# A drain written in another order, 54 transposes of the identity in it, and single PSUM banks behind it

## The chip, the cores and the metric

The kernel runs on one core of one Trainium2 chip. The metric is the device time of one execution in microseconds (us). Five engines work side by side, each through its own instructions in its own order: TensorE (PE, whose weight loads show as PEld), VectorE (DVE), ScalarE (ACT), GpSimd (POOL) and SyncE (SP), which here only issues DMAs. Matmul results lie in PSUM, 8 banks of 128 x 512 fp32; everything else lies in SBUF.

## The reference

Two attentions per head, then a mixture of experts with soft routing. N = 8 x 576 = 4608 rows of 512 come out of the attention, 32 slots go to 8 experts, 4 slots each.

```python
def sm_attn(qq, kk, vv):
    s = scale * np.matmul(qq, kk.transpose(0, 1, 3, 2))
    s = s - np.max(s, axis=-1, keepdims=True)
    a = np.exp(s)
    a = a / (np.sum(a, axis=-1, keepdims=True) + 1e-09)
    return np.matmul(a, vv)
p_packed = sm_attn(p, k, v)                # 8 batches, 8 heads, 32 x 64
x = sm_attn(q, p_packed, p_packed)         # 8, 8, 576 x 64 -> 4608 x 512
...
logits = x @ phi                           # 4608 x 32
d = np.exp(logits - logits.max(0, keepdims=True))
d /= d.sum(0, keepdims=True) + 1e-09       # softmax over the 4608 rows
slot_input = (d.T @ x).reshape(E, S_per_e, D)
for e in range(E):
    slot_out[e] = np.maximum(slot_input[e] @ w1[e], 0.0) @ w2[e]
c = np.exp(logits - logits.max(1, keepdims=True))
c /= c.sum(1, keepdims=True) + 1e-09       # softmax over the 32 slots
return (c @ slot_out.reshape(n_slots, D)).astype(np.float32)
```

## The kernel before

The attention runs in 8 steps i: double batch dd = i // 2 (two batches side by side on the 128 partitions) and head group g = i % 2. x is never formed: a step leaves the second attention's weights `a2`, and the logits come out of them and a small product of the packed values and phi. The names in the order, with the lines of the profile:

- `S2` and the scores s (L418, L430, a step's 72 matmuls); `MS`, `E2`, `Z`, `N2` the softmax: maximum (L457), difference (L458), exponent (L467), sum and reciprocal (L473 to L475), product (L480, on POOL or DVE); `MP` (L361) makes the small product with phi.
- `A2P` transposes `a2` on PE (L491) and `A2T` copies it (L502, L504); `LG` the logits lp (L518), `LT` keeps or adds them (L532, L535). The last step's softmax and transposes are cut in two (`E20`, `E21`, `A2P0`, `A2P1` and so on).
- Per double batch the softmax over rows runs on, with a running maximum and sum: `F1` maximum mt (L541), `F2` its transpose mx (L548), `F2d` new maximum m and difference dm (L555 to L568), `F3` two broadcasts my (L575, L583), `F3d` nmg (L588), `F3x` exponents dL and al (L594, L597), `F4d` two DVE transposes dz and rw (L604, L606), `F4` the sum mz (L611), `F5` the logits' transposed copy into `L_sb` (L614), `GZ` the running sum z_run and its rescaling of S_run (L624 to L636).
- `GR`: 36 matmuls gr of dz with `a2` (L654; a row of the order counts 18, the trace 36). `RTa` and `RTd` copy the result to rt on ACT and DVE (L667, L669), `GT` 16 more (L677), `GB` the product rb with the heads' mask (L688), `GS` (L710), `GSA` adds to S_run (L730). For the last double batch the sum goes to xz (L921), the experts' input.

`ORDER` (from L825) is a hand-written table of these names; inside `manual_schedule` each engine among PE, DVE, ACT and POOL keeps the order in which the table issues its work, and waits there in place. So an instruction that waits holds back all that follows it on its engine. SP is not in it: loads go out when their slot of the ring (14 slots of 1 MiB, and 7 extra ones) is free; weights are 32 pieces of 1 MiB. A step's `S2.7`, `F5.3` and `GR.3` also free the room for some of them, and the later ones wait for the experts to use up earlier ones.

Behind xz the experts run: `layer1a` (hp, L982, on 8 weight pieces for four experts), `hidden` (hs, L999, L1001), `layer1b` (ht, L1010), `layer2` (so, L1031); the last expert in halves (`last2`, sb, L1108), then sr (L1121, L1129) and sh (L1131, L1132). Beside them the combine weights are made from `L_sb`: maximum cm (L937), difference, exponent (L946), sum (L949), reciprocal, product (L952); nine groups `cp` of four transposes (L1062) bring them into the form cT. At the end 36 outputs: a matmul op (L1145, L1162), a copy to ob or ot by ACT (L87) or DVE (L90), and stores over SP (L1164, L1169, L1178). `evac` gives a copy to the engine with less on its account. PSUM is dealt out by pools: `pair` gives two banks under one name, `bank` one. In the attention `psm` holds one pair and `prs` three; behind it `psa` holds two pairs (hp, sb, sr, op), `pso` one bank (so), `pstr` three (ht, cp).

Behind the last step a drain is left: the logits of the last step, the softmax and gr of double batches 2 and 3.

Of the kernel before, what the change touches and what calls it, by code (L numbers as in the profile page):

```python
# [20 lines left out]
def pack_attention_soft_moe(  # L21
# [522 lines left out]
    def f2(dd):  # L544

        x = du[dd]
        bm = x["bm"] = pair(prs, f"mx_{dd}")[:, 0]
        nc.tensor.transpose(bm[0:1, 0:P], x["mt"], ident)  # L548
# [190 lines left out]
    def load_w(pool, lay, e, c):  # L739
# [92 lines left out]
        XQA.2 PREP.2 N2.1 MP.2 MXb.3 MM.2 S1a.3 EXb.3 MXa.3 QC.2 A2P.1 XQC.2 EXa.3 KT1.4 A2T.1
        S2.2 KT0.4 QE.3 AP.3 MT.2 MS.2 AT.3 A1T.3 LG.1 A1U.3 QC.3 PPM.3 XQC.3 E2.2 LT.1 F1.0
        F2.0 PPN.3 QA.3 F2d.0 QB.3 XQA.3 Z.2 F3.0 S1a.4 XQB.3 S1b.4 F3d.0 MXa.4 N2.2 F3x.0 F4d.0
        EXa.4 PT.3 MXb.4 PPT.3 F4.0 GR.0 QE.4 KT0.5 EXb.4 PRP.3 MP.3 RTa.0 AP.4 MM.3 PREP.3
        RTd.0 GZ.0 A1T.4 GT.0 KT1.5 S2.3 GB.0 GS.0 MT.3 AT.4 GSA.0 A2P.2 F5.0 A1U.4 MS.3 PPM.4
        A2T.2 QC.4 LG.2 E2.3 PPN.4 QB.4 LT.2 QE.5 Z.3 PT.4 XQC.4 XQB.4 QA.4 XQA.4 S1a.5 N2.3
# [373 lines left out]
```

## Time and profile before

| what | value |
|---|---|
| time, median of 3 runs | 240.16 us (239.95 to 242.99) |
| the profiled execution: time, span | 241.48 us, 239.7 us |
| PE busy | 192.1 us, 80% of the span |
| DVE, ACT, POOL busy | 137.5, 89.7, 31.2 us |
| DMA moved | 72.84 MB, mean 304 GB/s |
| HBM read, written | 62.98 MB, 9.44 MB |
| mean granted clock of PE | 0.876 |

The page gives busy times per engine and in 40 slices, the chain of work that ended last, and groups of instructions by line. A matmul's time is given up to its modelled end, so a PE that looks busy may be waiting inside its row of matmuls. [...]

### The profile page before, as it was taken

The page shows a single profiled execution, that of the slowest core. Times are in us where ns is not written, and L with a number is a line of the kernel's source. Part 1 is how long each engine was busy: PE and PEld are TensorE (multiplying, and loading weights), DVE is VectorE, ACT ScalarE, POOL GpSimd, SP SyncE. Part 2 cuts the span into 40 slices and gives each one's busy share as a digit, 9 for nine tenths or more (in the row PEclk, how much of TensorE's full clock was granted, in tenths as well). Part 3 has the DMA queues.
Part 4 walks back from the last instruction along what each step waited for, and adds up shares of the span by engine and source line. Part 5 has one row for each costly group of instructions (what it writes and reads, how often), then busy time and mean ns, then how long its engine had stood idle before and what let it go on. Part 6 is the DMA issues. An engine that isn't in the chain of part 4 may idle for free.

```text
span 239.7 us, 6484 instructions
## 1 busy us (share of the span) xinstructions
PE 192.1 (80%) x2795; PEld 128.6 (54%) x2795; DVE 137.5 (57%) x280; ACT 89.7 (37%) x174; POOL 31.2 (13%) x42
## 2 busy tenths in 40 slices
PE   0569977899879999979998627874999999688960
PEld 0247666777649777769786515772233344233320
DVE  2563786678596689767776486396312634433240
ACT  2041736374472473643667332102020010444520
POOL 6103000521060030020223010100030000000000
PEclk9999999999997999979999995757899999855555
DMA  5999999999999999995592990086499992278767
GB/s 155 385 338 349 390 391 270 390 389 326 345 389 391 391 406 407 407 374 187 198 355 72 424 383 5 0 299 228 130 421 428 418 415 118 72 282 347 298 278 304
DMA packets 27037, 72.84 MB, mean 304 GB/s; under 512 B 6400, under 2 KB 6656, under 8 KB 24192
## 3 DMA queue, kind: packets, MB, share of 16 engines
q1 hardware_dynamic: 27008, 72.42, 81.7%
q8 instruction: 22, 0.36, 0.6%
q14 instruction: 7, 0.06, 0.1%
HBM read 62.98 MB, written 9.44 MB: 302 GB/s over the span
## 4 chain that ended last, share of the span: by engine, by line
PE 52%; DMA 18%; DVE 14%; ACT 8%; issue 3%; SPq 1%; POOL 0%; DVEq 0%; ACTq 0%
DMA pn<-in_p_dram 8%; PE gr L654 7%; PE hp L982 7%; DMA k<-in_k_dram 6%; PE op L1145 6%; PE so L1031 5%; PE m L297 5%; PE s L430 4%; PE s L229 4%; DMA q<-in_q_dram 4%; PE a2p L491 3%; PE ap L263 2%; DVE ob L90 2%; ACT ob L87 2%; DVE kT L212 2%
## 5 line engine op out<-in xcount | busy, mean ns | idle before, releaser
L229 PE MATMUL s<-kT,pT 32*32 32x288 f32 x512 | 20.7, 458 | 9.2 <-DVE kT L212 8.7
L1145 PE MATMUL op<-sh,cT 128*128 128x512 f32 x35 | 23.1, 744 | 2.9 <-DVE ob L90 1.3
L480 POOL TENSOR_TENSOR a<-a,z 128x1152 f32<-128x1152 f32 (+1 forms) x8 | 15.9, 1992 | 61.7 <-DVE nmg L588 19.0
L212 DVE STREAM_TRANSPOSE kT<-k 128x1152 f32<-128x1152 f32 x16 | 21.4, 1358 | 0.2
L297 PE MATMUL m<-v,a1T 64*64 64x128 f32 x576 | 19.8, 291 | 0.7 <-ACT a1T L287 0.4
L250 ACT ACTIVATE a<-s,nm 128x576 f32<-128x576 f32 x16 | 11.9, 742 | 19.5 <-DVE nm L240 13.4
L297 PEld LDWEIGHTS m<-v,a1T 64*64 64x64 f32 x576 | 17.5, 144 | 3.1 <-issue 1.2
L240 DVE TENSOR_REDUCE nm<-s 128x1 f32<-128x576 f32 x16 | 12.0, 755 | 11.1 <-PE s L229 11.1
L1145 PEld LDWEIGHTS op<-sh,cT 128*128 128x128 f32 x35 | 9.8, 279 | 15.8 <-ACT ob L87 7.3
L386 PE MATMUL qp<-ident,q 128*128 128x128 f32 x128 | 16.7, 276 | 1.2 <-issue 1.2
L229 PEld LDWEIGHTS s<-kT,pT 32*32 32x32 f32 x512 | 9.0, 111 | 15.6 <-DVE kT L212 9.6
L90 DVE COPY ob<-op 128x512 f32<-128x512 f32 (+1 forms) x13 | 8.6, 670 | 14.0 <-PE op L1145 13.5
L87 ACT COPY ob<-op 128x512 f32<-128x512 f32 (+1 forms) x20 | 11.4, 575 | 13.5 <-PE op L1145 11.7
L654 PE MATMUL gr<-a,dz 128*64 128x128 f32 x144 | 16.4, 398 | 0.0
L982 PE MATMUL hp<-w,xz 128*32 128x512 f32 x128 | 16.0, 649 | 0.5 <-DVE xz L921 0.5
L430 PE MATMUL s<-ppT,qT 128*64 128x64 f32 x512 | 16.3, 222 | 0.1
L391 ACT COPY qT<-qp 128x1024 f32<-128x1024 f32 x16 | 15.9, 1021 | 0.7 <-PE qp L386 0.6
L386 PEld LDWEIGHTS qp<-ident,q 128*128 128x128 f32 x128 | 14.0, 141 | 3.3 <-issue 2.7
L654 PEld LDWEIGHTS gr<-a,dz 128*64 128x64 f32 x144 | 15.2, 206 | 1.1 <-issue 0.9
L430 PEld LDWEIGHTS s<-ppT,qT 128*64 128x64 f32 x512 | 15.6, 138 | 0.2 <-ACT a L250 0.2
L491 PE MATMUL a2p<-ident,a 128*128 128x128 f32 x64 | 9.7, 296 | 5.5 <-POOL a L480 4.5
L457 DVE TENSOR_REDUCE mx<-s 128x32 f32<-128x1024 f32 (+1 forms) x9 | 9.9, 1096 | 6.0 <-PE s L430 6.0
(144 smaller groups left out, 283.0 us busy)
## 6 DMA issues: line engine op xcount, KB each, us to landing
w<-in_moe_w_dram SPq DMA_DIRECT2D x31, 1024.0 KB, 10.7
k<-in_k_dram SPq DMA_DIRECT2D x16, 576.0 KB, 8.4
v<-in_v_dram SPq DMA_DIRECT2D x16, 576.0 KB, 10.3
q<-in_q_dram SPq DMA_DIRECT2D x16, 576.0 KB, 11.6
out_dram<-ob SPq DMA_DIRECT2D x7, 1024.0 KB, 3.9
pn<-in_p_dram SPq DMA_DIRECT2D x16, 64.0 KB, 8.0
w<-in_moe_w_dram SPq DMA_DIRECT2D x2, 512.0 KB, 16.9
out_dram<-ot SPq DMA_DIRECT2D x2, 512.0 KB, 5.3
```

The source lines that it names most:

```text
L87: nc.scalar.copy(dst, src)
L212: nc.vector.transpose(st[i]["kT"][:, b2].rearrange("p a t x r -> p (a t x r)"), kts[i][:, b2].rearrange("p a x -> p (a x)"),)
L229: nc.tensor.matmul(ps[32 * c : 32 * c + 32, u, 0:HALF], pTs[dd][rs, b2, g, a, x], kT[rs, b2, a, :, x, :], start=(x == 0), stop=(x == 1),)
L297: nc.tensor.matmul(s["m"][64 * b2 : 64 * b2 + 64, y, 0:P], s["a1T"][rs, t, 64 * b2 : 64 * b2 + 64], vt[rs, b2, :, t * D : (t + 1) * D], st ...
L386: nc.tensor.transpose(tp[:, o : o + P], qts[i][:, b2, a, j * P : (j + 1) * P], ident)
L391: nc.scalar.copy(flat(qT(i)[:, 8 * b2 : 8 * b2 + 8]), st[i][f"qp{b2}"])
L430: nc.tensor.matmul(pv[64 * b2 : 64 * b2 + 64, j, h], s["qT"][:, 8 * b2 + 4 * a + j, R * y : R * y + R], ppT[:, b2, h], start=True, stop=True,)
L480: eng.tensor_tensor(a2, a2, st[i][f"z{t0}"].unsqueeze(3).broadcast_to([P, n, 4, NS]), op=ALU.mult)
L491: nc.tensor.transpose(s["ap2"][:, t * P : (t + 1) * P] if t < 8 else s["lp"][:, 1, 0:P], s["a2"][:, t].rearrange("p h s -> p (h s)"), ident,)
L654: nc.tensor.matmul(x["gb"][64 * c : 64 * c + 64, g * P : (g + 1) * P], dz[:, t].rearrange("p b s -> p (b s)"), a2[:, t].rearrange("p h s - ...
L982: nc.tensor.matmul(hp[nh][32 * a : 32 * a + 32, :], xzf[:, (4 * e + a) * NSLOT : (4 * e + a + 1) * NSLOT], w1s[e, a // 2][:, a % 2, nh * 5 ...
L1145: nc.tensor.matmul(op, cT[:, o, :], sh, start=True, stop=True)
```

## The change

1. `ORDER`. For double batches 0 and 1, `F3` to `F4d` go ahead of `QB`, `Z` and the next `MX`, and `GR` ahead of `F4`. For double batch 2, `F2` to `F4d` go ahead of `MP.7` to `MT.7`, `GR.2` right behind `S2.7`, `GT.2` ahead of `A2P0.7`, `GS.2` ahead of `LG.7`, all of it ahead of `F1.3`; `mz` takes its bank from `psm`. For double batch 3, `GR.3` goes ahead of `F4.3` and `GZ.3`.
2. `fill(x, o)`: PE transposes of the identity into a part of a PSUM bank that nobody reads, at six places (`GT.2` 12, `F2.3` 11, `F3.3` 7, `GR.3` 12, `GT.3` 6, `GS.3` 6). Those at GR, GT and GS write the second bank of the pair whose first bank gr uses.
3. The maximum cm of the combine weights is tied behind xz.
4. hp, sb, sr and op take single banks out of `pstr`, which grows from 3 to 7; `psa` goes.

```diff
+    FILL = {("GT", 2): 12, ("F2", 3): 11, ("F3", 3): 7, ("GR", 3): 12, ("GT", 3): 6, ("GS", 3): 6}
+
+    def fill(x, o):
+        for _ in range(FILL.get(x, 0)):
+            nc.tensor.transpose(o, ident, ident)
...
         bm = x["bm"] = pair(prs, f"mx_{dd}")[:, 0]
+        fill(("F2", dd), bm[:, P : 2 * P])
...
         bm = x["bn"] = pair(prs, f"my_{dd}")[:, 0]
+        fill(("F3", dd), bm[:, 0:P])
...
-        x["zp"] = pair(prs, f"mz_{dd}")[:, 0, 0:NSLOT]
+        if dd == ND - 2:
+            mz = psm.tile([P, 2, 512], F32, tag="m", name=f"mz_{dd}")
+        else:
+            mz = pair(prs, f"mz_{dd}")
+        x["zp"] = mz[:, 0, 0:NSLOT]
...
-            x["gb"] = pair(prs, f"gr_{dd}")[:, 0]
+            gp = pair(prs, f"gr_{dd}")
+            x["gb"], x["gf"] = gp[:, 0], gp[:, 1, 0:P]
+            fill(("GR", dd), x["gf"])
...
     def gt(dd):
+        fill(("GT", dd), du[dd]["gf"])
...
         x["gs"] = x["gb"]
+        fill(("GS", dd), x["gf"])
...
-        GT.2 F2d.3 F3.3 GB.2 GS.2 F3d.3 F3x.3 GSA.2 F4d.3 F4.3 F5.3 GZ.3 GR.3 RTa.3 RTd.3 GT.3
+        F2.3 F2d.3 F3.3 F3d.3 F3x.3 F4d.3 F5.3 GR.3 F4.3 GZ.3 RTa.3 RTd.3 GT.3 GB.3 GS.3 GSA.3
...
-        psa = ctx.enter_context(tc.tile_pool(name="psa", bufs=2, space=psum))
         pso = ctx.enter_context(tc.tile_pool(name="pso", bufs=1, space=psum))
-        pstr = ctx.enter_context(tc.tile_pool(name="pstr", bufs=3, space=psum))
+        pstr = ctx.enter_context(tc.tile_pool(name="pstr", bufs=7, space=psum))
...
-        nc.vector.tensor_reduce(cm[:, a:b], Lf[:, a:b], axis=AX.X, op=ALU.max)
+        top = nc.vector.tensor_reduce(cm[:, a:b], Lf[:, a:b], axis=AX.X, op=ALU.max)
+        tc.add_manual_dep(
+            top.ins,
+            xz_add.ins.name,
...
-            hp = pair(psa, f"hp_{e0}")
-            hss[e0] = [hp[:, 0], hp[:, 1]]
+            hss[e0] = [bank(pstr, f"hp_{e0}_{nh}") for nh in range(2)]
...
-    def slot_out(dst, n, o, x):
-        if x == 0:
-            ops[0] = pair(psa, f"op_{n}")
-        op = ops[0][:, x]
+    def slot_out(dst, n, o):
+        op = bank(pstr, f"op_{n}")
         nc.tensor.matmul(op, cT[:, o, :], sh, start=True, stop=True)
```

What this does to the engines' orders, at three places. First PE around the end of step 7's scores (L430), before; `gr` are the matmuls of GR, `a2p` and `lp` transposes and logits of steps 6 and 7, `my` and `mx` the broadcasts and the transposed maximum. The first two rows are S2.7, the last is F2.3:

```order
L418 MATMUL m_1902<-ppT,qT_1915 64x2x32 x4
L430 MATMUL s_7_2050<-ppT,qT_1915 64x2x32 x32
L575 MATMUL my_2099<-ones,m_2_2030 128x1
L583 MATMUL my_2099<-dm_2032,ones 128x32
L518 MATMUL lp_2039<-a2T_2093,mm_1814 32x288 x4
L491 MATMUL a2p_2132<-ident,a_7_2049 128x128 x8
L491 MATMUL lp_2133<-ident,a_7_2049 128x128
L611 MATMUL mz_2153<-rw_2148,ones 128x32
L518 MATMUL lp_2133<-a2T_2139,mm_2036 32x288 x4
L654 MATMUL gr_2163<-a_4_1350,dz 64x128 x9
L654 MATMUL gr_2163<-a_5_1628,dz 64x128 x9
L548 MATMUL mx_2188<-ident,mt_2186 1x128
```

And the same place after (line numbers of the changed file: gr L670, fills L211, mz L625, GT L693):

```order
L426 MATMUL m_1902<-ppT,qT_1915 64x2x32 x4
L438 MATMUL s_7_2064<-ppT,qT_1915 64x2x32 x32
L670 MATMUL gr_2116<-a_4_1350,dz 64x128 x9
L670 MATMUL gr_2116<-a_5_1628,dz 64x128 x9
L526 MATMUL lp_2053<-a2T_2110,mm_1814 32x288 x4
L625 MATMUL mz_2149<-rw_2050,ones 128x32
L211 MATMUL gr_2116<-ident 128x128 x12
L693 MATMUL gr_2116<-repb,rt_2117 64x32 x8
L499 MATMUL a2p_2184<-ident,a_7_2063 128x128 x8
L499 MATMUL lp_2185<-ident,a_7_2063 128x128
```

The 36 gr matmuls of double batch 2 have moved from behind the logits of step 7 (the second `lp`) to directly behind the scores; my (now ahead of MP.7, outside these rows) no longer stands behind them; mz, the 12 fills and GT stand ahead of step 7's transposes.

Second, PE at the end of the drain, in the changed kernel, with the semaphores that each row waits for: from the fills ahead of the last gr (GR.3) to GT.3 and GS.3:

```order
L211 MATMUL gr_2265<-ident 128x128 [waits PE_49]
L211 MATMUL gr_2265<-ident 128x128 x11
L670 MATMUL gr_2265<-a_6_1843,dz 64x128 [waits DVE_49]
L670 MATMUL gr_2265<-a_6_1843,dz 64x128 x8
L670 MATMUL gr_2265<-a_7_2063,dz 64x128 x9
L625 MATMUL mz_2306<-rw_2256,ones 128x32 [waits DVE_49,PE_49]
L211 MATMUL gr_2265<-ident 128x128 [waits DVE_49]
L211 MATMUL gr_2265<-ident 128x128 x5
L693 MATMUL gr_2265<-repb,rt_2278 64x32 x8
L211 MATMUL gr_2265<-ident 128x128 [waits DVE_49]
L211 MATMUL gr_2265<-ident 128x128 x5
L727 MATMUL gr_2265<-rb_2279,ppd_1751 64x64 x2
```

The fills at GR wait for PE's own earlier work alone. Those at GT and GS wait for DVE: for its copy of gr to rt, and for rb, as the tile to which they write is the pair that holds gr. mz stands behind gr.

Third, DVE at the end of the drain, before (z_run, hm, al and S_run are GZ.3, cm and L_sb the combine weights, rt and rb RTd.3 and GB.3):

```order
L937 TENSOR_REDUCE cm<-L_sb 128x36
L625 TENSOR_TENSOR z_run<-z_run,mz_2228 128x32
L938 TENSOR_TENSOR L_sb<-L_sb,cm 128x1152
L627 TENSOR_SCALAR z_run<-z_run 128x32
L628 RECIPROCAL z_run<-z_run 128x32
L629 TENSOR_TENSOR hm<-hm,z_run 128x64
L635 TENSOR_TENSOR al_2221<-al_2221,z_run 128x32
L636 TENSOR_TENSOR S_run<-S_run,al_2221 128x128
L669 COPY rt_2245<-gr_2244 128x128
L949 TENSOR_REDUCE cm<-L_sb 128x36
L688 TENSOR_TENSOR rb_2246<-gr_2244,hm 128x128 x2
L950 TENSOR_SCALAR cm<-cm 128x36
```

And after:

```order
L638 TENSOR_TENSOR z_run<-z_run,al_2252 128x32
L639 TENSOR_TENSOR z_run<-z_run,mz_2306 128x32
L641 TENSOR_SCALAR z_run<-z_run 128x32
L642 RECIPROCAL z_run<-z_run 128x32
L643 TENSOR_TENSOR hm<-hm,z_run 128x64
L649 TENSOR_TENSOR al_2252<-al_2252,z_run 128x32
L650 TENSOR_TENSOR S_run<-S_run,al_2252 128x128
L685 COPY rt_2278<-gr_2265 128x128
L704 TENSOR_TENSOR rb_2279<-gr_2265,hm 128x128 x2
L937 TENSOR_TENSOR xz<-S_run,gr_2265 128x8x4x4
L952 TENSOR_REDUCE cm<-L_sb 128x36
L959 TENSOR_TENSOR L_sb<-L_sb,cm 128x1152
```

The rows of GZ.3 stand ahead of the copy rt as before, but mz, which they wait for, now comes after gr; cm has gone behind xz.

More of the change, by code (lines that the diff above doesn't have):

```diff
@@ L832, in pack_attention_soft_moe @@
[L832 to L837, printed above, removed]
@@ new lines, in pack_attention_soft_moe @@
+        AT.3 A1T.3 LG.1 A1U.3 QC.3 PPM.3 XQC.3 E2.2 LT.1 F1.0 F2.0 PPN.3 QA.3 F2d.0 F3.0 XQA.3 F3d.0
+        QB.3 F3x.0 Z.2 F4d.0 S1a.4 XQB.3 S1b.4 MXa.4 N2.2 EXa.4 PT.3 MXb.4 PPT.3 GR.0 F4.0 QE.4
+        KT0.5 EXb.4 PRP.3 MP.3 RTa.0 AP.4 MM.3 PREP.3 RTd.0 GZ.0 A1T.4 GT.0 KT1.5 S2.3 GB.0 GS.0
+        MT.3 AT.4 GSA.0 A2P.2 F5.0 A1U.4 MS.3 PPM.4 A2T.2 QC.4 LG.2 E2.3 PPN.4 QB.4 LT.2 QE.5 Z.3
+        PT.4 XQC.4 XQB.4 QA.4 XQA.4 S1a.5 N2.3 PPT.4 S1b.5 MXa.5 MP.4 EXa.5 MXb.5 MM.4 A2P.3 EXb.5
+        KT1.6 S2.4 A2T.3 KT0.6 AP.5 MT.4 MS.4 AT.5 A1T.5 LG.3 A1U.5 QC.5 PPM.5 QE.6 XQC.5 E2.4 LT.3
@@ new lines, in pack_attention_soft_moe @@
+        F1.1 F2.1 PPN.5 QA.5 F2d.1 F3.1 XQA.5 F3d.1 QB.5 F3x.1 Z.4 F4d.1 S1a.6 XQB.5 S1b.6 MXa.6
+        N2.4 EXa.6 PT.5 MXb.6 PPT.5 GR.1 F4.1 KT0.7 EXb.6 MP.5 RTa.1 AP.6 MM.5 RTd.1 GZ.1 GT.1 A1T.6
+        S2.5 KT1.7 GB.1 GS.1 MT.5 AT.6 GSA.1 A2P.4 F5.1 A1U.6 MS.5 PPM.6 A2T.4 QC.6 LG.4 E2.5 PPN.6
+        QE.7 QA.6 LT.4 Z.5 PT.6 XQC.6 QB.6 PPT.6 XQA.6 MP.6 S1a.7 MM.6 XQB.6 N2.5 S1b.7 MXa.7 S2.6
+        EXa.7 MXb.7 EXb.7 QA.7 MT.6 MS.6 AT.7 AP.7 A1U.7 XQA.7 QC.7 A1T.7 E2.6 A2P.5 PPM.7 XQC.7 Z.6
@@ L936, in c1 @@
     def c1(a, b, eng=nc.vector):
-        nc.vector.tensor_reduce(cm[:, a:b], Lf[:, a:b], axis=AX.X, op=ALU.max)
+        top = nc.vector.tensor_reduce(cm[:, a:b], Lf[:, a:b], axis=AX.X, op=ALU.max)
+        tc.add_manual_dep(
+            top.ins,
+            xz_add.ins.name,
+            mybir.DependencyInfo(mybir.DependencyClass.NoSync, mybir.DependencyReason.SCHED_ONLY),
+            reason="the experts' inputs go first",
+        )
         eng.tensor_tensor(
@@ L1095, in pack_attention_soft_moe @@
         halves = [slice(x * DM // 2, (x + 1) * DM // 2) for x in range(2)]
-        sb2 = pair(psa, "sb")
-        sb = [sb2[:, x] for x in range(2)]
+        sb = [bank(pstr, f"sb{x}") for x in range(2)]
         so2 = extras[0].tile([P, 2, DM], F32, tag="ring", name="sot")
@@ L1102, in pack_attention_soft_moe @@
         shf = sh.bitcast(F32)
-        sr2 = pair(psa, "sr")
-        srs = [sr2[:, 0], sr2[:, 1]]
+        srs = [bank(pstr, f"sr{x}") for x in range(2)]
         repf = rep.rearrange("p c s -> p (c s)")
@@ L1157, in pack_attention_soft_moe @@
                 if (dd, o) == (0, 0):
-                    op0 = pair(psa, "op_0")
-                    for x, (xs, eng) in enumerate(zip(halves, ("act", "dve"))):
-                        op = op0[:, x]
+                    for xs, eng in zip(halves, ("act", "dve")):
+                        op = bank(pstr, f"op_0_{eng}")
                         nc.tensor.matmul(op[:, xs], cT[:, k_, :], sh[:, xs], start=True, stop=True)
@@ L1174, in pack_attention_soft_moe @@
                     cp(todo.pop(0), None)
-        slot_out(ot[:, dd], f"{dd}", dd * T + T - 1, (dd == 0))
+        slot_out(ot[:, dd], f"{dd}", dd * T + T - 1)
     for y in range(2):
```

30 lines of the change are left out of this document (11 added, 19 removed).

## The prediction

> **What bounds the kernel now.** I read the page first, then a table of windows cut where the granted clock changes, then the chain of waits, and last the timeline around the stages that the change touches. From the page: the span, one group of output copies and the output stores.
>
> ```profile
> span 239.7 us, 6484 instructions
> ...
> L90 DVE COPY ob<-op 128x512 f32<-128x512 f32 (+1 forms) x13 | 8.6, 670 | 14.0 <-PE op L1145 13.5
> ...
> out_dram<-ob SPq DMA_DIRECT2D x7, 1024.0 KB, 3.9
> ```
>
> The profiled execution took 241.48 us, 1.78 us more than its span, and 1.32 us more than the median of the three timed runs (240.16). I sum against the profiled execution and take 1.32 off at the end.
>
> The windows give, for each stretch, the busy time of each engine, then the granted clock, the DMA share and the GB/s.
>
> ```profile
> core 0: us, PE busy (x) PEld busy (x) DVE busy (x) ACT busy (x) POOL busy (x), PEclk, DMA share, GB/s
> 132.49:135.90 3.41, 2.09 (x28) 1.46 (x28) 2.39 (x9) 0.94 (x3) 0.00 (x0) 1.00 1.02 430
> ...
> 139.31:142.73 3.42, 0.10 (x4) 0.00 (x0) 3.28 (x10) 2.10 (x5) 0.00 (x0) 1.00 1.00 405
> 142.73:152.97 10.24, 7.93 (x54) 6.48 (x55) 5.11 (x13) 1.52 (x6) 2.10 (x2) 0.50 0.08 30
> ...
> 156.38:163.20 6.82, 5.06 (x38) 4.63 (x38) 5.42 (x14) 0.59 (x2) 0.00 (x0) 0.50 0.85 307
> ...
> 170.03:201.39 31.36, 31.26 (x304) 13.03 (x302) 10.30 (x23) 3.32 (x6) 2.06 (x2) 1.00 0.91 369
> 201.39:205.78 4.39, 2.47 (x21) 1.11 (x19) 1.28 (x3) 1.49 (x4) 0.00 (x0) 1.00 0.00 0
> 205.78:239.70 33.92, 23.25 (x36) 9.88 (x36) 10.01 (x15) 12.15 (x21) 0.00 (x0) 0.53 0.70 279
> ```
>
> Three stages follow each other. From 139 to 167 is the drain: PE idles 3.32 of 3.42 us, and the next three windows of 3.41 us run at half clock. From 170 to 201 the experts' weights arrive at a DMA share of 0.91; PE looks full there; I read that as matmuls that are paced by their weights. From 205.78 on the outputs leave at 0.70 of the DMA engines, with PE at half clock.
>
> The chain of waits, around the scores of the second double batch and in the drain (start, duration, work):
>
> ```profile
> 99.39 1.27 DVE z L473
> ...
> 101.33 0.64 ACT dL L594 x2
> ...
> 102.96 0.63 DVE rw L606
> 103.72 0.38 PE mz L611 x2
> 104.10 3.40 PE gr L654 x36
> ...
> 116.56 1.02 PE qp L386 x8
> ...
> 148.94 4.33 PE gr L654 x36
> 153.93 0.68 PE gr L677 x16
> ...
> 157.46 0.60 PE mz L611 x2
> 158.06 4.47 PE gr L654 x36
> ...
> 163.97 1.35 DVE cm L949
> 165.33 0.41 DVE rb L688 x2
> 165.78 0.47 PE gr L710 x8
> ```
>
> The same view from 160 us to the end, for the first expert matmul and the rhythm of the outputs:
>
> ```profile
> 166.69 10.46 PE hp L982 x80
> ...
> 217.13 0.81 PE op L1145
> 217.96 0.59 ACT ob L87
> 218.60 0.81 PE op L1145
> ```
>
> And the timeline rows of the drain to which I attach the change:
>
> ```profile
> 134.52 0.33 PE L361 MATMUL m<-phi_sb,ppT 64*32 64x32 f32 x16
> ...
> 135.12 0.18 DVE L566 TENSOR_TENSOR dm<-m_run,m 1x32 f32<-1x32 f32 x1
> ...
> 142.84 1.05 POOL L480 TENSOR_TENSOR a<-a,z 128x512 f32<-128x512 f32 x1 [10.71 <-ACT dL L594]
> ...
> 143.94 1.11 PE L491 MATMUL a2p<-ident,a 128*128 128x128 f32 x4 [4.53 <-POOL a L480]
> ...
> 149.57 0.45 DVE L541 TENSOR_REDUCE mt<-LT 128x1 f32<-128x288 f32 x1
> ...
> 153.18 0.27 PE L548 MATMUL mx<-ident,mt 128*1 128x128 f32 x1
> ...
> 156.10 0.96 DVE L604 STREAM_TRANSPOSE dz<-dL 64x288 f32<-64x288 f32 x2
> ...
> 159.00 0.18 DVE L625 TENSOR_TENSOR z_run<-z_run,mz 128x32 f32<-128x32 f32 x1
> ...
> 161.35 0.29 DVE L636 TENSOR_TENSOR S_run<-S_run,al 128x128 f32<-128x128 f32 x1
> ```
>
> **The middle (double batches 0 and 1).** nmg moves ahead of z, and gr ahead of mz. In the chain, z at 99.39 stands ahead of dL at 101.33, and mz (0.38) directly ahead of gr at 104.10. Without mz gr gains 0.38; with dL no longer behind z it gains perhaps 0.5 more, until DVE's other work ends last. I take 0.9 for each of the two, 1.75 in all; from 0.5 (PE has other work queued) to 2.7 (a half-clock window also goes).
>
> **The drain.** Five steps.
>
> First, the broadcast my of double batch 2 now stands before MP.7. Its input dm is ready at 135.30 (the row at 135.12), and my itself takes about 0.35, so MP.7 starts near 135.65 and not at 134.52; S2.7, the 64 matmuls behind it, also ends 1.1 later, near 139.3, where the idle window begins.
>
> Second, the 36 gr matmuls of double batch 2 come right behind S2.7, into the window in which PE is busy 0.10 of 3.42 us: 3.40 us by the row at 104.10, to about 142.8. Before, they stood at 148.94 and took 4.33. Two things follow. The window is no longer idle, so I expect the half clock from 142.73 not to come. And F2.3's transpose at 153.18, whose input mt was ready at 150.0, no longer queues behind them. ACT's rt copy and LG.6, queued behind gr, have slack; the xz memset moves ahead of the POOL pass at 142.84, whose engine was idle 10.71 us.
>
> Third, the 12 fills ahead of GT.2. Their tile is that of gr, so the first waits for DVE's copy of gr (rt), the one for which GT.2 waits. They run behind the wait, in front of GT.2 and of the a2p transposes. Eight qp transposes took 1.02 (116.56, full clock); with 0.27 for a lone one (mx at 153.18, also full) each further one costs 0.75 / 7 = 0.107, and twice that, 0.21, at half clock. I take 0.107: 1.28 us for 12. With the 1.1 from above, a2p goes from 143.94 to about 145.8. From there to mt the chain was 5.63 us at half clock, with a2p twice (1.11), lp, two copies; at full clock PE's part shrinks by about 1.4, so mt starts near 150.1 and F2.3 near 150.75.
>
> Fourth, from F2.3 to the end of dz was 3.88 us, 153.18 to 157.06, with GT.2 and GS.2 of double batch 2 between; those are gone from there, so 3.45: dz ends at 154.2. gr then starts at 154.25, because mz (0.60) now follows it: it was 158.06. F2.3's 11, F3.3's 7 and GR.3's 12 fills wait only for PE's own work; they run in the waits for mt, for dm and for dz, over 0.5 us each, and cost up to 0.3 together.
>
> Fifth, what is late next. gr ends at 157.65 (full clock; 158.7 half). mz comes after it (0.38), and the DVE chain from z_run to S_run, 2.64 us between 159.00 and 161.64 with two foreign operations of 1.35 in it, so about 1.4, has lost gr as its cover and stands ahead of rt. rt then ends near 159.8. Six fills (0.64), GT (0.68), rb (0.41), six more fills behind it (0.64), GS (0.47) and the 0.44 from GS's end at 166.25 to hp at 166.69 follow: hp near 163.1. The 1.35 of cm, which held rb at 165.33, has been tied behind xz and costs nothing there. So hp starts 3.5 us sooner than 166.69; 2.2 if the clock is half for part of it.
>
> **The experts.** They are bound by the weights:
>
> ```profile
> 170.28 14.23 SPq L753 DMA_DIRECT2D w<-in_moe_w_dram  x12
> ```
>
> The first of these 12 loads waits for hp to finish an expert, 3.59 us after hp began. SP's order is the same. With hp starting 3.5 to 2.2 sooner, and if the clock is full by then up to half of the 3.59 less behind it, the loads start 2.3 to 5.2 sooner; I take 4. Against that, 28 cp transposes, which filled PE's weight waits near 195, now stand in the outputs. The 4.39 us behind the last weights ran at full clock; at half they would be up to 1.8 longer, and I take 0.7. Drain and experts: 4.0 - 0.7 = 3.3 us.
>
> **The outputs.** Two pairs of banks before: two matmuls, then a wait for the older copy, 1.47 us per 512 KB (217.13 to 218.60). Seven single banks take that wait away; what is late next is the stores. A share of 0.70 of 33.92 us is 23.7 us of full DMA work. To it I add 1.5 for the start, with its small stores, and 0.8 to 2.5 for the last landing (a median 3.9 from issue, part of it already counted): 26.0 to 27.7. PE's part:
>
> ```profile
> 197.61 0.80 PE L1062 MATMUL cp<-identr,c 128*128 128x128 f32 x7
> ...
> 217.13 1.22 PE L1145 MATMUL op<-sh,cT 128*128 128x512 f32 x2 [0.25 <-DVE ob L90]
> ```
>
> The second of two op costs 1.22 - 0.81 = 0.41 at half clock, 36 of them 14.8; 28 cp at twice 0.114 are 6.4. That is 21.2, under 23.7. ACT and DVE share 36 copies and 7 cT casts at 0.59 (217.96) and 0.67: 13.5 each. So 6.2 to 7.9 us go; I take 7.0.
>
> **The sum.** 241.48 - 1.75 - 3.3 - 7.0 = 229.4 for a profiled execution, 228.1 as a median. The small terms at their ends give 225 to 231.5.
>
> **What speaks against it: do transposes hold the clock?** In 132.49 to 135.90 PE ran small matmuls, most of them transposes, for 2.09 of 3.41 us, and the next window was still full. No window holds transposes alone, so that is weak. [...]
>
> **The rivals.**
>
> A, the forecast, 228.1: chance 0.58.
>
> B, the drain stays at half clock. For it: 156.38 to 163.20 is half although PE was busy 5.06 of 6.82 us there, with gr. Then fills cost 0.21 each, gr 4.47, and the 24 fills behind their waits 5.1 us. mt then starts near 151.6, dz ends at 156, gr at 160.5, mz, DVE and rt at 162.9; fills, GT, rb, fills, GS and xz (1.28, 0.68, 0.41, 1.28, 0.47, 0.44) bring hp to 167.5, 0.8 later than now, and the loads too. With the middle at 1.3 and the outputs at 6.5: 240.16 - 1.3 + 0.8 - 6.5 = 233.2. Chance 0.20.
>
> C, the outputs keep a rhythm of their own: a copy and the next matmul still alternate, since cp and cT now stand among them, and only 2 us go. 240.16 - 1.75 - 3.3 - 2 = 233.1. For it: PE's 21.2 is near DMA's 23.7, and PE may stall in front of each cp. Chance 0.12.
>
> D, all terms at their good ends: 240.16 - 2.7 - 5.2 - 7.9 = 224.4. Chance 0.07.
>
> E, slower: all fills of a group write the same 128 columns of PSUM. If each waited for the one before, it would cost its whole latency, 0.27 by the lone transpose mx at 153.18, and up to twice that at half clock. To lose 4.8 us net, the fills must eat 12.05 + 4.8 us and the 2.9 that the sum gives them, 19.8: 0.37 each with all 54 exposed, or 0.82 if only the 24 behind their waits count. Against it: gr accumulates 9 matmuls on the same columns and still takes 3.40 / 36 = 0.094 each. At 0.42 each and all exposed, 22.7 us against the 2.9 of the sum: about 248. Chance 0.03.
>
> That the change does not do what it says is true of the 24 fills at GT and GS, which stand behind their waits; the sum holds it, 2.56 us at 0.107.
>
> **The numbers.** 228.1 is A's. From 223.8 to 235 the range holds A, C, D for the most part and B to 1.8 us above its centre; left out are E, a third of B, and the outer ends of A, C and D, not quite 0.2. A measurement here tells about 2% from no change, 4.8 us: faster is below 235.4, slower above 245. A, D, nearly all of C and two thirds of B are faster, 0.89; the rest of B and C lies within, 0.08; E is slower, 0.03.
>
> **What would show it.** In the profile after: the granted clock full from 139 to 156 (else B); the gr group of double batch 2 ending near 142.8; F2.3's mx near 150.8; gr at 154.3; the first fill of GT at the end of the rt copy, not before; hp near 161.4 (163.1 less the middle's gain); the loads' first issue near 164.5; the stretch from the first store to the end 26 to 28 us with a DMA share over 0.85. The forecast is wrong if that share stays near 0.7, if fills are spaced more than 0.2 us, or if hp starts later than 165.

## The result and the profile after

The changed kernel took 230.12 us (median of 4 runs, 228.05 to 234.16), the kernel before, run beside it, 240.69 us (239.95 to 242.99). The ratio is 0.9517, with a 95% interval from 0.9413 to 0.962: about 11 us less. A median here is over all executions of a kernel, a ratio only over those within 1.5% of its fastest, so the two can differ by a us. The forecast was 228.1, in a range from 223.8 to 235.

The profiled execution after took 230.18 us, with a span of 228.4. Its windows, cut where the granted clock changes (busy time of PE, PEld, DVE, ACT and POOL with the number of instructions, granted clock, DMA share, GB/s):

```profile
core 0: us, PE busy (x) PEld busy (x) DVE busy (x) ACT busy (x) POOL busy (x), PEclk, DMA share, GB/s
...
129.29:132.70 3.41, 0.71 (x3) 0.28 (x3) 2.75 (x8) 0.75 (x3) 0.51 (x1) 1.00 0.98 413
132.70:139.53 6.83, 6.63 (x89) 6.20 (x91) 2.33 (x9) 2.11 (x6) 0.00 (x0) 0.50 0.86 361
...
149.77:153.18 3.41, 3.41 (x32) 3.10 (x29) 1.98 (x7) 0.26 (x1) 0.00 (x0) 1.00 0.62 183
...
156.59:160.01 3.42, 1.65 (x17) 1.20 (x14) 1.54 (x7) 0.27 (x1) 0.00 (x0) 1.00 0.84 332
160.01:163.42 3.41, 2.83 (x30) 2.36 (x30) 0.49 (x2) 0.00 (x0) 0.00 (x0) 0.50 0.68 263
163.42:167.40 3.98, 3.53 (x26) 1.06 (x26) 2.91 (x3) 0.64 (x1) 0.00 (x0) 0.57 0.01 4
...
202.55:228.40 25.85, 11.12 (x63) 8.08 (x62) 11.96 (x20) 11.51 (x23) 0.00 (x0) 0.80 0.91 365
```

Three things are to be seen. From 139.5 to 160 the clock is full, where it had been half for most of the time. Two stretches are half that the forecast had full: 132.70 to 139.53, behind a window in which PE was busy 0.71 us, and 160.01 to 166.83, behind one with 1.65 (the row from 163.42 to 167.40 holds its end and a little full clock). And the outputs take 25.85 us at a DMA share of 0.91, instead of 33.92 at 0.70.

The timeline of the drain and its surroundings after (start, duration, line, operation); L211 are the fills, L349 the transposes of step 7's ppd, L585 the first broadcast my, L670 is gr, L693 the matmuls of GT:

```profile
130.91 0.44 PE L349 MATMUL m<-ident,ppd 128*128 128x128 f32 x2 [1.78 <-DVE ppd L334]
...
131.85 0.27 PE L557 MATMUL mx<-ident,mt 128*1 128x128 f32 x1 [0.50 <-DVE mt L549]
...
132.90 0.55 PE L585 MATMUL my<-ones,m 1*128 1x1 f32 x2 [0.78 <-DVE m L572]
...
136.82 3.27 PE L438 MATMUL s<-ppT,qT 128*64 128x64 f32 x64
...
139.92 2.35 PE L670 MATMUL gr<-a,dz 128*64 128x128 f32 x36
...
144.00 0.23 DVE L685 COPY rt<-gr 128x128 f32<-128x128 f32 x1
...
144.29 1.53 PE L211 MATMUL gr<-ident 128*128 128x128 f32 x12 [1.06 <-DVE rt L685]
...
151.10 0.27 PE L557 MATMUL mx<-ident,mt 128*1 128x128 f32 x1
...
154.60 2.40 PE L670 MATMUL gr<-a,dz 128*64 128x128 f32 x36 [0.45 <-DVE dz L614]
...
158.77 0.28 DVE L685 COPY rt<-gr 128x128 f32<-128x128 f32 x1
...
159.10 0.87 PE L211 MATMUL gr<-ident 128*128 128x128 f32 x6 [1.77 <-DVE rt L685]
159.91 1.02 PE L693 MATMUL gr<-repb,rt 128*64 128x32 f32 x16
...
161.51 1.54 PE L211 MATMUL gr<-ident 128*128 128x128 f32 x6 [0.58 <-DVE rb L704]
...
164.13 2.81 PE L1002 MATMUL hp<-w,xz 128*32 128x512 f32 x12 [0.45 <-DVE xz L937]
```

and SP's own rows, with the first of the twelve weight loads that wait for the experts and the first output store:

```profile
167.40 14.88 SPq L771 DMA_DIRECT2D w<-in_moe_w_dram  x12
202.55 0.83 SPq L1177 DMA_DIRECT2D out_dram<-ob  x2
```

The same events before and after, in us from the start of the span, with what the forecast had for the difference (a sum of its terms up to there):

| event | before | after | difference | forecast |
|---|---|---|---|---|
| mx of double batch 2 | 134.19 | 131.85 | -2.3 | -1.75 |
| end of step 7's scores (S2.7) | 138.2 | 140.1 | +1.9 | -0.65 |
| mx of double batch 3 | 153.18 | 151.10 | -2.1 | -4.2 |
| gr of double batch 3 | 157.99 | 154.60 | -3.4 | -5.5 |
| hp | 166.69 | 164.13 | -2.6 | -5.3 |
| first of the 12 loads | 170.28 | 167.40 | -2.9 | -5.75 |
| first output store | 205.78 | 202.55 | -3.2 | -5.05 |
| end of the span | 239.70 | 228.40 | -11.3 | -12.05 |

So the outputs gave 8.1 and everything ahead of them 3.2. From mx of double batch 2 to hp, the drain itself took 32.28 us instead of 32.50: 0.2 less, where the forecast counted 3.5.

### The profile page after: what moved, and what is told of

The parts are those of the page before. It is cut to its first block, busy times and chain, and to the rows that moved or that the text cites. A ratio compares the mean times of both kernels' runs of the same rounds, so it can differ in the third digit from the quotient of the medians.

```text
span 228.4 us, 6597 instructions
## 1 busy us (share of the span) xinstructions
PE 179.2 (78%) x2849; PEld 126.1 (55%) x2849; DVE 139.1 (61%) x280; ACT 88.0 (39%) x174; POOL 31.2 (14%) x42
## 5 line engine op out<-in xcount | busy, mean ns | idle before, releaser
L438 PE MATMUL s<-ppT,qT 128*64 128x64 f32 x512 | 17.6, 231 | 0.1
L438 PEld LDWEIGHTS s<-ppT,qT 128*64 128x64 f32 x512 | 16.9, 147 | 0.2 <-ACT a L258 0.2
L1051 PE MATMUL so<-w,hT 128*32 128x512 f32 x112 | 12.7, 594 | 1.4 <-DMA w<-in_moe_w_dram 1.4
L481 DVE TENSOR_REDUCE z<-a 128x36 f32<-128x1152 f32 (+2 forms) x9 | 10.9, 1210 | 1.9 <-ACT a L475 1.9
L475 ACT ACTIVATE a<-a 128x1152 f32<-128x1152 f32 (+2 forms) x9 | 9.5, 1061 | 6.3 <-DVE a L466 5.4
L287 ACT COPY a1T<-ap 128x1024 f32<-128x1024 f32 x8 | 8.1, 1018 | 8.3 <-PE ap L271 8.3
L271 PE MATMUL ap<-ident,a 128*128 128x128 f32 x64 | 9.7, 296 | 1.7 <-ACT a L258 1.2
L510 ACT COPY a2T<-a2p 128x1024 f32<-128x1024 f32 (+1 forms) x9 | 8.3, 919 | 6.2 <-PE a2p L499 6.2
```

What stands on the lines that cost most here:

```text
L438: nc.tensor.matmul(pv[64 * b2 : 64 * b2 + 64, j, h], s["qT"][:, 8 * b2 + 4 * a + j, R * y : R * y + R], ppT[:, b2, h], start=True, stop=True,)
L481: nc.vector.tensor_reduce(z, a2, axis=AX.X, op=ALU.add)
L1051: nc.tensor.matmul(so[32 * a : 32 * a + 32, :], hTf[:, (NJ * e + j) * NSLOT : (NJ * e + j + 1) * NSLOT], w2s[e, j // 4][:, j % 4, :], star ...
```

## The experiments

Two accounts stood against each other. One is the forecast's: banks free the outputs until the DMA bounds them; the order shortens the drain; 30 fills hold the clock in their waits; 24 fills stand behind their waits and cost what they take. The other: the fills, being transposes, do not hold the clock, or the outputs gained for another reason than the banks. Each kernel was timed in 6 executions beside executions of the kernel before on the same chip.

**The banks alone.** The kernel before with this part of the diff only:

```diff
-        psa = ctx.enter_context(tc.tile_pool(name="psa", bufs=2, space=psum))
-        pstr = ctx.enter_context(tc.tile_pool(name="pstr", bufs=3, space=psum))
+        pstr = ctx.enter_context(tc.tile_pool(name="pstr", bufs=7, space=psum))
...
-        op = ops[0][:, x]
+        op = bank(pstr, f"op_{n}")
```

> The kernel before with the single banks alone: hp, sb, sr and op out of seven single banks, the order and the waits of the drain as before, no fills. My account (the outputs are bound by the DMA once the banks are free): first output store within 1 us of before's 205.8, the stretch from it to the end 26 us instead of 33.9 with a DMA share of 0.9, time about 8 us under before (232.5). Rival (the outputs gained in the changed kernel mostly because PE came into them at full clock, which the drain and the new place of the cp transposes brought): the stretch stays near 30 us, time 236 to 237.

It took 233.27 us, ratio 0.9706 (0.9657 to 0.9756): 7 us less. The row of the output stretch in its windows:

```profile
204.53:231.10 26.57, 11.11 (x63) 8.07 (x62) 11.97 (x20) 11.51 (x23) 0.00 (x0) 0.74 0.89 356
```

26.57 us at a share of 0.89, with the drain and its order as before. The first store came 1.25 us sooner than before, a little more than expected. The rival falls: by these traces at most 0.7 of the outputs' gain is left for anything else.

**The order alone.** The changed kernel with `FILL = {}` and the old pairs of banks behind xz; the tie of cm stays in.

> The changed kernel with its new order and the tie of cm, but with the old pairs of banks behind xz and without the 54 fills. My account: the middle gives 2.3, the drain about 1 to 2 without fills, the outputs nothing: first output store at 202 to 203, output stretch 33 to 34, time about 3 us under before (237.5). Rival (the order gains nothing unless the fills hold the clock): time within 1 us of before.

238.8 us, ratio 0.990 (0.9854 to 0.9946): 1.7 us less by the medians, 2.4 by the ratio. That is a little under the 3 that I expected, and not the rival's nothing. Its outputs took 33.61 us at a DMA share of 0.70, as before.

**Without the fills.**

```diff
-    FILL = {("GT", 2): 12, ("F2", 3): 11, ("F3", 3): 7, ("GR", 3): 12, ("GT", 3): 6, ("GS", 3): 6}
+    FILL = {}
```

> The changed kernel without the 54 fills. My account: the 24 fills that stand behind their waits cost 3.9 us of PE on the path, the 30 others keep the clock full for gr of the last double batch (2.4 us against 4.5 at half); the two nearly cancel, so hp starts within 1 us of 164.1 and the time is within 1.5 us of the changed kernel's 230. Rival 1 (fills pay): gr at half clock and more half-clock windows behind it, time 232 to 234. Rival 2 (fills only cost): clock as with them, time 226 to 227.

232.06 us, ratio 0.9645 (0.9597 to 0.9693), against 0.9517 (0.9413 to 0.962) with them. That is 1.9 above the changed kernel by the medians, 0.4 outside my 1.5 and at the edge of rival 1. The two intervals overlap at 0.96, so that the 54 fills pay where they stand in the changed kernel is likely, not shown. In the trace without them the clock is half from 148.93 to 162.58, and gr of double batch 3 takes 4.31 us instead of 2.40.

**The fills out of the pair of gr.** The counts stay; the 24 fills at GT and GS write a bank that nothing in front of them still reads:

```diff
             mz = psm.tile([P, 2, 512], F32, tag="m", name=f"mz_{dd}")
+            x["mf"] = mz[:, 1, 0:P]
...
-        fill(("GT", dd), du[dd]["gf"])
+        fill(("GT", dd), du[2]["mf"] if dd > 1 else None)
...
-        fill(("GS", dd), x["gf"])
+        fill(("GS", dd), du[2]["mf"] if dd > 1 else None)
```

> The changed kernel, with the 24 fills at GT and GS written to the second bank of the pair that holds mz of double batch 2, so that they no longer wait for rt and rb; the counts are the same. My account: they run in the waits for rt and rb, hp starts 2 to 3 us sooner than in the changed kernel (161 to 162), time 227 to 228. Rival (the wait of DVE's chain was the limit and the fills hid behind other work): time within 0.7 us of the changed kernel.

226.61 us, ratio 0.9399 (0.9356 to 0.9442): 3.5 us under the changed kernel by the medians. The intervals touch, but all six executions (224.39 to 227.83) lie under all four of the changed kernel (228.05 to 234.16). Its timeline at the end of the drain:

```profile
155.62 0.85 PE L211 MATMUL mz<-ident 128*128 128x128 f32 x6
...
157.22 0.28 DVE L686 COPY rt<-gr 128x128 f32<-128x128 f32 x1
...
157.56 0.66 PE L694 MATMUL gr<-repb,rt 128*64 128x32 f32 x16 [1.09 <-DVE rt L686]
158.14 0.87 PE L211 MATMUL mz<-ident 128*128 128x128 f32 x6
158.26 0.49 DVE L705 TENSOR_TENSOR rb<-gr,hm 128x128 f32<-128x128 f32 x2 [0.76 <-PE gr L694]
...
159.85 4.52 PE L1003 MATMUL hp<-w,xz 128*32 128x512 f32 x40 [0.45 <-DVE xz L938]
```

The first six fills end at 156.47, before rt does, and GT follows rt at once; in the changed kernel GT came 0.86 behind rt's end. hp stands at 159.85 instead of 164.13; part of that is the clock, which is full from 138.72 to 189.92 here. What the forecast read from the order, that these fills run behind their waits and not in them, is shown.

**Only the 30 fills that can hide.** The three entries of GT and GS are taken out of the table.

> The changed kernel with only the 30 fills at F2.3, F3.3 and GR.3; the 24 at GT and GS are gone. If the 24 only cost (they run behind their waits): hp 3.5 us sooner than in the changed kernel and the time that of the kernel with the fills in the waits, 226.6. If they also hold the clock (without them the window around GT.2 is busy for about 1.2 of 3.4 us): half clock from about 146 to 153, which costs 1.5 to 2.5 us of the 3.9 that they took, time 228 to 229.

229.48 us, ratio 0.9481 (0.9423 to 0.9538). That is 0.6 under the changed kernel, not told apart: behind their waits the 24 take about as much (3.9 us in the changed kernel's trace) as the clock that they hold there is worth. It is 2.9 above the kernel in which the 24 run in their waits, by the medians; these intervals overlap a little (0.9423 to 0.9442). Its windows show what happens without them, half clock from 146.32 to 153.15 as expected, and one thing more:

```profile
142.91:146.32 3.41, 1.70 (x26) 1.24 (x22) 3.24 (x9) 1.19 (x3) 1.05 (x1) 1.00 0.48 196
146.32:149.73 3.41, 2.93 (x21) 1.64 (x21) 1.80 (x8) 1.18 (x3) 0.00 (x0) 0.50 0.00 0
149.73:153.15 3.42, 3.42 (x20) 3.20 (x17) 1.29 (x4) 0.00 (x0) 0.00 (x0) 0.50 0.62 177
153.15:156.56 3.41, 2.97 (x27) 2.52 (x27) 2.01 (x8) 0.71 (x3) 0.00 (x0) 1.00 0.33 135
```

and PE's timeline in the third of them:

```profile
149.87 2.61 PE L211 MATMUL mx<-ident 128*128 128x128 f32 x11
152.27 0.42 PE L557 MATMUL mx<-ident,mt 128*1 128x128 f32 x1
152.49 1.25 PE L211 MATMUL my<-ident 128*128 128x128 f32 x7
```

The window without fills (1.70 busy) is followed by half clock. The window from 149.73 to 153.15 holds 0.2 us of the end of logits matmuls, and then 16 transposes and nothing else; it is at half clock, and the next is full. Here the clock did not only stay full behind transposes, it rose from 0.50 to 1.00 behind them.

**GZ ahead of GR again.**

```diff
-        F2.3 F2d.3 F3.3 F3d.3 F3x.3 F4d.3 F5.3 GR.3 F4.3 GZ.3 RTa.3 RTd.3 GT.3 GB.3 GS.3 GSA.3
+        F2.3 F2d.3 F3.3 F3d.3 F3x.3 F4d.3 F5.3 F4.3 GZ.3 GR.3 RTa.3 RTd.3 GT.3 GB.3 GS.3 GSA.3
```

(with the 12 fills of GR still ahead of both).

> The changed kernel with F4.3 and GZ.3 ahead of GR.3 again (the 12 fills of GR stay ahead of both), so that DVE's chain from z_run to S_run lies beside gr. My account: gr starts 0.6 later (behind rw and mz), DVE's 1.4 us and mz are off the path, rt 0.8 sooner; time 0.5 to 1 us under the changed kernel. Rival (DVE's chain was not on the path, or the later gr eats it): no difference.

227.16 us, ratio 0.9434 (0.9382 to 0.9486): 3 us under the changed kernel by the medians, more than the 0.5 to 1 expected, though the two intervals overlap (0.9413 to 0.9486). Its timeline:

```profile
157.00 2.40 PE L672 MATMUL gr<-a,dz 128*64 128x128 f32 x36
...
157.11 0.19 DVE L642 TENSOR_TENSOR z_run<-z_run,mz 128x32 f32<-128x32 f32 x1
...
158.29 0.29 DVE L653 TENSOR_TENSOR S_run<-S_run,al 128x128 f32<-128x128 f32 x1
...
159.79 0.29 DVE L687 COPY rt<-gr 128x128 f32<-128x128 f32 x1 [1.20 <-ACT rt L685]
160.13 0.87 PE L211 MATMUL gr<-ident 128*128 128x128 f32 x6 [0.74 <-DVE rt L687]
...
162.19 0.87 PE L211 MATMUL gr<-ident 128*128 128x128 f32 x6 [0.59 <-DVE rb L706]
...
163.89 1.08 PE L1004 MATMUL hp<-w,xz 128*32 128x512 f32 x8 [0.45 <-DVE xz L939]
```

DVE's chain lies beside gr. From the end of dz (156.28) to the end of rt (160.08) it takes 3.80 us; in the changed kernel 4.51 (154.54 to 159.05). That is the 0.7 I had counted, and with it the rival, that the chain was not on the path, falls. Behind rt the two traces differ by the clock: from rt's end to hp 3.81 instead of 5.08 us, since the second six fills take 0.87 and not 1.54 and GT is at full clock too. That the order of GZ is what kept the clock full there is not shown.

**Fourteen fills ahead of step 7's transposes of ppd.** On the kernel with the fills in their waits, into the window of PE's 1.8 us wait for DVE that put the scores of step 7 at half clock:

```diff
+        if i == NSTEP - 1:
+            x = du[i // NG - 1]
+            x["mx"] = pair(prs, f"mx_{i // NG - 1}")
+            fill(("PT", i), x["mx"][:, 0, P : 2 * P])
```

> The kernel with the fills in their waits (226.6) and 14 more ahead of the two transposes of ppd in step 7, where PE waits 1.8 us for DVE; the window from about 128.5 to 131.9, which held only 8 matmuls and 3 transposes, then holds mostly transposes. If transposes hold the granted clock: it stays full from there to 139, the scores of step 7 take 1.9 and not 3.3 us, hp 1.5 to 2.5 us sooner, time about 225. If they do not count (rival B): half clock from 131.9 as before, time 226.5 to 227.

222.85 us, ratio 0.9223 (0.917 to 0.9276): 3.8 under the kernel it builds on, more than the 1.5 to 2.5 expected, and the intervals lie apart. The profiled execution is not one that shows why. It took 226.57 us, and its clock did not stay full up to 139:

```profile
133.22:136.63 3.41, 2.12 (x17) 1.48 (x15) 2.66 (x10) 0.73 (x2) 0.03 (x1) 1.00 1.00 420
```

This window, with ten of the 14 fills, was followed by half clock to 140.05. With 6 more fills in the wait for m it stayed full, as the trace of everything together shows, below.

**The cp groups back in the waits for the last weights.** On the same base, `layer2` is called with the groups that go ahead of its last pieces:

```diff
-        layer2(2, E - 1)
+        layer2(2, E - 2)
+        layer2(E - 2, E - 1, (8, 12), (16, 20))
...
+        for t0 in (24, 28, 32):
+            cp(t0, None)
...
-    todo = list(range(8, NT, 4))
+    todo = []
```

> The kernel with the fills in their waits (226.6), in which PE starved for the last weights and fell to half clock from 190 to 197; here the seven cp groups of the outputs go into the waits for the last four weight pieces, as the scheduler had them before the change. My account: the clock stays full there, from the last weight's landing to the first store 2 us less; the outputs, bound by the DMA, take the same 25.9 us; time about 224.7. Rival (the outputs need the cp groups' spacing, or the so matmuls come later behind the cp): no difference or slower.

226.34 us, ratio 0.9356 (0.93 to 0.9411), against 226.61 and 0.9399 (0.9356 to 0.9442): not told apart. The traces differ as expected. The kernel with the fills in the waits, from its first ring load to its first store, and the part of it at half clock:

```profile
161.80:199.24 37.44, 33.79 (x291) 12.85 (x284) 14.04 (x33) 4.90 (x9) 2.08 (x2) 0.91 0.76 309
...
189.92:196.75 6.83, 5.81 (x36) 2.46 (x36) 0.42 (x1) 0.37 (x1) 0.00 (x0) 0.50 0.15 61
```

and the same stretch with the cp groups in the waits:

```profile
165.00:199.96 34.96, 33.90 (x319) 14.30 (x312) 16.73 (x37) 6.66 (x12) 2.08 (x2) 1.00 0.81 331
```

2.5 us less there, in one execution of each. But the changed kernel's own trace, with the cp groups in the outputs, has 35.15 us for this stretch, at full clock too. Why the medians do not show a gain is open: whether the window in which PE starves falls so that the clock drops may differ between executions of one kernel, which a single trace of each cannot tell.

**The middle.** The kernel before with the new order of double batches 0 and 1 alone:

> The kernel before with the new order of double batches 0 and 1 alone (F3 to F4d earlier, GR ahead of F4); the drain, the fills and the banks as before. If the middle gives what the changed kernel's trace shows at the transposed maximum of double batch 2 (2.3 us sooner), the time is 2 us under before, 238.5 to 239, as much as the whole new order without fills gave. Rival (the drain takes it back, since the windows of the clock then fall otherwise): within 0.7 us of before.

241.66 us with a spread from 237.03 to 251.16, unclear. In its profiled execution, that of 251.16, the granted clock was 0.95, neither full nor half, where the other traces have 1.00; its mean was 0.838, against 0.863 to 0.895 in the other five, and in the chain of waits eight qp transposes took 1.13 us, against 1.02 in the kernel before. So the middle was put to the test from the other side, the changed kernel with the old order of these two:

> The changed kernel with the old order for double batches 0 and 1 alone; drain, fills and banks as changed. If the middle is worth the 2.3 us by which the changed kernel's trace is ahead at the transposed maximum of double batch 2: 232 to 232.5. Rival (worth nothing at the end, as the run of the middle alone, at 241.7 and widely spread, would have it): 229.5 to 230.5.

231.56 us, ratio 0.9636 (0.9589 to 0.9684), 1.4 above the changed kernel by the medians, 2.9 by the ratios. The intervals overlap (0.9589 to 0.962). In its profiled execution (229.3) mx of double batch 2 comes at 133.94, 2.1 later than in the changed kernel's, but hp at 163.56, 0.6 sooner, since only one window was half at step 7's scores and none at the last fills. So what the middle is worth at the end, in the changed kernel or in the kernel before, is not settled.

**All together.** The fills out of the pair of gr, 14 ahead of ppd and 6 ahead of my of double batch 2, GZ ahead of GR with 4 fills each at GT.3 and GS.3, once with the cp groups in the weights' waits and once without.

> All that gained: the fills at GT and GS out of the pair of gr, 14 fills ahead of step 7's ppd transposes and 6 ahead of my of double batch 2, F4.3 and GZ.3 ahead of GR.3 with 4 fills each at GT.3 and GS.3, and the cp groups in the waits for the last weights. Added up from 226.6: 3.8 for the fills at ppd, 0.5 to 1 for GZ (the other 2 of its gain lay in the clock, which is full there already), 0 to 1 for cp: 221 to 222. If the gains overlap (each one only saved the same half-clock windows): no better than the kernel with the fills at ppd, 222.9.

> The same combination, but with the cp groups left in the outputs as in the changed kernel. If the half clock in the waits for the last weights costs: 1 to 2 us slower than the combination. If not, the same within 0.7 us.

223.23 us, ratio 0.9203 (0.9149 to 0.9257), and 223.88 us, ratio 0.9179 (0.9105 to 0.9253). They are 17 us under the kernel before and 6 to 8 under the changed one, but not better than the kernel with 14 fills ahead of ppd (222.85, 0.9223). The two are not told apart either, so the 1 to 2 us that the second was expected to lose did not show. The gains overlap: GZ's extra had lain in the clock, and in the second's trace, with all of them, the clock is full from 110.78 to 209.77. Which of them could then be left out was not tested. From mx of double batch 2 to hp both traces take 24.67 us, against 32.28 in the changed kernel. In the trace of the second, around step 7's scores:

```profile
131.26:134.67 3.41, 2.87 (x23) 2.16 (x21) 2.71 (x10) 0.73 (x2) 0.07 (x1) 1.00 1.01 425
134.67:138.09 3.42, 3.42 (x91) 3.17 (x92) 1.83 (x6) 2.11 (x6) 0.00 (x0) 1.00 1.00 424
```

and in PE's timeline:

```profile
130.59 1.75 PE L211 MATMUL mx<-ident 128*128 128x128 f32 x14
132.44 0.44 PE L353 MATMUL m<-ident,ppd 128*128 128x128 f32 x2
133.29 0.27 PE L561 MATMUL mx<-ident,mt 128*1 128x128 f32 x1 [0.41 <-DVE mt L553]
133.40 0.82 PE L211 MATMUL my<-ident 128*128 128x128 f32 x6
...
136.48 2.04 PE L442 MATMUL s<-ppT,qT 128*64 128x64 f32 x64
```

A window in which 19 of the 23 instructions are transposes is followed by full clock, and the 64 score matmuls take 2.04 us instead of 3.27.

## Why the prediction was right, point by point

The time lies 2.0 us above the forecast and inside its range, and it is the case A that happened. But that it lies so near is partly luck, as terms were mis-sized in opposite ways: the drain, from mx of double batch 2 to hp, gave 0.2 us instead of 3.5, the middle 2.3 instead of 1.75, hp to the first store 0.7 instead of a loss of 0.2, the outputs 8.1 instead of 7.0.

**The middle.** 1.75 was forecast, and at mx of double batch 2 the trace shows 2.3. The order did what I counted: from mx to gr of double batch 1 it takes 5.98 us (95.51 to 101.49) instead of 7.09 (96.94 to 104.03), 1.1 where I had 0.9, and the run with the old middle has 7.10. But how much of it arrives depends on the clock. From mx of double batch 0 to that of double batch 2 the changed kernel's trace took 68.10 us, with full clock all the way, instead of 70.42; the traces of the 14 fills and of everything without cp, with the same new middle and three half-clock windows in between, took 71.18 and 71.29. That the 2.3 came in whole was in part luck.

**The drain, first step.** This is the step that failed. I let S2.7 end 1.1 us later because my of double batch 2 stands ahead of MP.7. Behind mx (131.85) it ended 8.2 us later, and before it had been 4.0. The wait for my was there, but I had not asked what the earlier middle and this wait do to the clock ahead of the drain: PE's waits for ppd, mt and m (1.78, 0.50 and 0.78 us) now fell together into one window (0.71 of 3.41 us busy), and the next two were half, so 64 score matmuls took 3.27 instead of the 2.04 of before, and the a2p ahead of them, too, ran at half.

```profile
136.19 2.04 PE L430 MATMUL s<-ppT,qT 128*64 128x64 f32 x64
```

The earlier middle alone is not the reason: in the run with the old middle the window from 132.35 to 135.76 held 1.48 us, and the next was half. Nor was the full clock of before safe. In the run of the banks alone, with the old order, the window from 132.10 to 135.52 held 1.91 us, against 2.09 before, and the next was half. The run with 14 fills in this wait gained 3.8 us, which prices it.

**The drain, second step.** gr went into the idle window behind S2.7 as said, and the clock stayed full behind it, also as said. I took 3.40 for it from a row of the middle; it took 2.35 to 2.40. The row that I used lay across a clock change (105.18), and the half-clock rows of 4.33 and 4.47 would have given 2.2 by halving.

**Third.** The 12 fills at GT began at the end of rt (144.29 behind 144.23) and took 1.53, where I had 1.28: spaced 0.109 in the trace, against the 0.107 counted, with the last one's 0.33 on top.

**Fourth.** With the 30 fills that wait only for PE the clock held: full from 149.77 to 160, where the trace without fills was half. dz was ready at 154.54 and gr followed it at 154.60, as the order without mz ahead of it promised.

**Fifth.** mz and DVE's chain had lost their cover and stood ahead of rt, as counted: gr's end to rt's end took 2.1 us, of which the run with GZ first got 0.7 back. The chain took 1.48 (157.37 to 158.85) where I had about 1.4, though I misread its row of before: only one foreign operation, not two, lay in those 2.64 us. cm no longer holds rb, which now follows GT at once; what its tie is worth alone no run tells. But the window from 156.59, with PE waiting for that chain, held only 1.65 us of work, and the last twelve fills and GT ran partly at half clock: 3.43 us for the three (0.87, 1.02, 1.54) where I had 1.96. I had named half clock for part of it as the poorer end (2.2 instead of 3.5); it was poorer still.

**The experts.** The first load came 3.3 us behind hp and the first store 35.2 behind it, against 3.6 and 35.5. hp began at half clock here; with the fills in the waits it began at full clock, and the first load came 1.95 behind it, near the half of 3.59 that I had allowed at best. The 0.7 for a colder end did not come in this trace; in that of the fills in the waits the clock was half from 189.92 to 196.75.

**The outputs.** I had 26.0 to 27.7 us for the stretch and it took 25.85; 8.1 gained, not 7.0. The DMA work was sized right: 0.91 of 25.85 is 23.5, against the 23.7 that I had taken from before. That leaves 2.3 us beside the DMA work, the low end of my 2.3 to 4.0 for the start and the last landing; which of the two was smaller I did not separate. PE's part, which I had at half clock and 21.2 us, was 11.12: with free banks the matmuls follow each other closely (from 204.38 to 211.21 PE is busy all of the 6.83 us) and the clock stays full until PE is done, 14.7 us ahead of the end. Rival C (a rhythm of copies) falls with this, and the run of the banks alone shows it without the rest.

**The signs.** Those that I had named for mx (150.8) and gr (154.3) of double batch 3 look met, with 151.10 and 154.60. But they left out the middle's 1.75 that the sign for hp takes off; with it both come over 2 us late, as the table has them, and hp and the first load come 2.7 and 2.9 behind their signs. The last six fills, at half clock, are spaced 0.21 us, just beyond the 0.2 that I had set.

**The rivals.** B has the drain stay at half clock in spite of the fills. That transposes do not hold the clock no run shows; two traces speak for the contrary: behind 15 fills and one other transpose, after a remainder of 0.2 us, the clock went from 0.50 to 1.00 (the 30 fills alone, 153.15), and behind a window with 19 transposes among 23 instructions it stayed at 1.00 (all together, 134.67). The row that I had set for B, half from 156.38 to 163.20, does not tell whether transposes hold the clock: it follows a window (152.97 to 156.38) with 2.15 us busy, and behind windows with 2.06 and 2.12, the second with ten fills in it, the clock was half too. In the window from 132.49 to 135.90, a weak sign against B, 12 of the 28 instructions were transposes, though they took most of the 2.09 us. The drain at half clock, B's outcome, did happen, but behind a window without fills and one with six. E falls by the rows: 12 fills in 1.53 us, whichever columns they write. That the 24 fills are not in the waits was right, and moving them there gave 3.5 us; the sum had priced them at 2.6, and in the trace they took 3.9 (1.53, 0.87 and 1.54), the last six at half clock.

My small terms at their poor ends add up to 231.9, not 231.5. Against the profiled execution the forecast's 229.4 is 0.8 short of 230.18: 2.85 too much for what lies ahead of the loads, 1.0 too little for the experts, 1.1 too little for the outputs. The other 1.2 of the 2.0 is that the profiled execution lay 1.32 above the median before, which I took off, and lies on the median now.

## What to carry to other kernels

In this kernel a wait is on a tile, not on its bytes, and decides when an instruction may start: the six fills at GT.3, written beside gr into the pair that rt is copied from, began at 159.10, behind the end of rt (159.05); written into another pair they ended at 156.47, before rt's copy on DVE began (157.22). So filler that is meant for a wait has to write something that nobody in front of the wait still reads, and the order with its semaphores tells this before any run. When waits are moved, look at what work is left between them, not only at the stage that is being shortened: here three waits fell into one window (0.71 of 3.41 us busy, 129.29 to 132.70), the clock behind it was half to 139.53, and the scores ahead of gr took 3.27 us instead of 2.04. And take a duration only from a row that lies on one side of a clock change: the 36 gr matmuls took 3.40 us across one, 2.35 to 2.40 at full clock and 4.47 at half.
